# Pooled q and k of batches 1 to 3: column sums on TensorE against a matrix of ones, instead of VectorE reductions and transposes

## The chip, the cores and the metric

One NeuronCore of one Trainium2 chip runs the kernel. The metric is the device time of one execution in microseconds; the time before is the median of three runs. The profile is of one further execution, read from the hardware profiler.

## The reference, cut to what matters

Inputs q, k, v have the shape (4 batches, 8 heads, 576 positions, 64). The output passes through an attention layer and two feed-forward layers; the change is in the attention's downsampled half:

```python
q_d = q.reshape(B, H, Sd, 4, D).mean(axis=3)      # Sd = 144
k_d = k.reshape(B, H, Sd, 4, D).mean(axis=3)
v_d = v.reshape(B, H, Sd, 4, D).mean(axis=3)
out_d = softmax(q_d @ k_d.T / 8) @ v_d
out_up = np.repeat(out_d, 4, axis=2)
...
x = (out_up + out_local) as (2304 tokens, 512)
h = x @ w_in;   y = (s * relu(h)**2 + b) @ w_out
h = y @ w2_in;  out = (h - tanh(h)) @ w2_out
```

out_local is a softmax over the seven nearest positions.

## The kernel before, in words

The 2304 tokens of the first feed-forward layer are cut into eight units of 288 (unit u is half a batch). For each unit, 16 chunks of the hidden width run on TensorE: layer 1 into the PSUM tile ph (line 735), relu, square and a split into two float32r parts on ScalarE and VectorE (tiles gh and gl, lines 747 to 756), and layer 2 into acc (line 768). Every float32 product is three float32r matmuls, so a chunk is 24 dense matmuls of 128 rows, 128 columns and 288 tokens. The second feed-forward layer follows (lines 735 and 1016) and touches nothing of this change.

Attention of batch 0 runs at the start in a form of its own. For batches 1 to 3 it runs beside the dense matmuls of the units before: `local_items` (the seven-wide half: products on VectorE, GpSimd and ScalarE, lines 181, 186, 245, 249 and 257, then transposes of O into the tile xt at line 296, the sum with the upsampled half at line 314, and the split into xh and xl) and `down_items` (the downsampled half). A unit's first dense matmul needs its xh.

`down_items(b)` walks four pairs of heads hq. For each pair:

- `load` (line 336) issues on SyncE's queue two DMAs each for q, k and v into a tile `raw`: 72 partitions, each with four neighbouring positions of two heads, in pieces of 1 KB. One pool of two buffers holds q, k and v in turn.
- `padd` (line 345) sums the four positions: for q and k one VectorE reduction over the innermost of a rearranged view (line 353), for v two additions on GpSimd (lines 350 and 351). The sums are the tiles pp.
- `qkt` (line 368) transposes each pp by TensorE in two halves of 72 (line 375) into the PSUM tile qkps, and ScalarE copies it to qkT (lines 379 and 380).
- `scores`, `norm`, `ptr` and `pvm` make the 144 by 144 softmax and its product with v (tiles S, E, PT and up; lines 391 to 444) and fill upT.

The PSUM tiles qkps, S, PT, up and xt take turns in one pool of two banks (tag sd).

The items of the two lists are laid into the chunks' slots in program order. Batch 1's run in the last 18 or so slots ahead of unit 2, those of batches 2 and 3 over two units each. Then `list_schedule` (line 1260) sets the order of every engine's instructions from a table of costs and due times, and `pin_order` fixes it: each engine, and SyncE's queue, runs strictly in that order. The table prices a float32 matmul that is no transpose at 1.2 ns a moving column, a transpose at 64 or 110 ns, and a dense one at (columns + 32) / 2.4 ns (lines 1084 to 1094); a DMA's bytes start 1.3 us after its issue, flow at 300 GB/s, and have landed 0.9 us later (lines 1316 to 1321).

Of the kernel before, what the change touches and what calls it, by code (L numbers as in the profile page):

```python
# [7 lines left out]
F32 = mybir.dt.float32  # L8
# [3 lines left out]
ALU = mybir.AluOpType  # L12
AX = mybir.AxisListType.X

B, H, S, D = 4, 8, 576, 64
# [10 lines left out]
GH = G // 2  # L26
# [52 lines left out]
def attention_moe_moe_kernel(ctx: ExitStack, tc, q, k, v, w_in, w_out, s_in, b_in, w2_in, w2_out, out):  # L79
    nc = tc.nc  # L80
    pe, act, dve, pool, sp = nc.tensor, nc.scalar, nc.vector, nc.gpsimd, nc.sync

    sb = ctx.enter_context(tc.tile_pool(name="sb", bufs=1))
# [17 lines left out]
    ident = sb.tile([128, 128], F32, name="ident")  # L101
    caps = [sb.tile([128, TAU, NO], F32, tag=f"cap{h}", name=f"cap{h}") for h in range(2)]
    scal = sb.tile([128, 2], F32, name="scal")
    bcol = sb.tile([128, KC], F32, name="bcol")

    def emit_consts():
        pool.memset(ident, 0.0)
        pool.affine_select(out=ident, in_=ident, pattern=[[-1, 128]], compare_op=ALU.not_equal,
                           fill=1.0, base=0, channel_multiplier=1)

        band = g_p.tile([128, NB1], F32, tag="gl", name="band")[:QB, :KW + 6]
        pool.memset(band, 0.0)
        pool.affine_select(out=band, in_=band, pattern=[[1, KW + 6]], compare_op=ALU.is_ge,
                           fill=-BIG, base=-3, channel_multiplier=-1)
        pool.affine_select(out=band, in_=band, pattern=[[-1, KW + 6]], compare_op=ALU.is_ge,
                           fill=-BIG, base=9, channel_multiplier=1)
        b0["band"] = start.tile([QB, 1, KW + 6], F32R, name="bandr")
        b0["id"] = start.tile([QB, QB], F32R, name="identr")
        act.copy(out=b0["band"][:, 0], in_=band)
        act.copy(out=b0["id"], in_=ident[:QB, :QB])  # L120

        pool.memset(caps[0], FREE)
        for t in range(3):
            pool.memset(caps[0][0:4, t, 0:3 - t], MASKED)
        pool.memset(caps[1], FREE)
        c = caps[1][96:128]
        pool.affine_select(out=c, in_=c, pattern=[[-1, TAU], [-1, NO]], compare_op=ALU.is_ge,
                           fill=MASKED, base=11, channel_multiplier=0)
        pool.affine_select(out=c, in_=c, pattern=[[0, TAU], [0, NO]], compare_op=ALU.is_ge,
                           fill=FREE, base=-28, channel_multiplier=1)  # L130
# [201 lines left out]
    def down_items(b):  # L332
        it = []
        st = {}

        def load(hq):
            for nm, a in (("q", q), ("k", k), ("v", v)):
                base = (b * H + 2 * hq) * S * D
                t = raw_p.tile([128, 2, 2, 4, D], F32, tag="raw", name="raw72")
                for hf in range(2):  # L340
                    src = bass.AP(a.tensor, base + hf * GH * 4 * D, [[4 * D, GH], [S * D, 2], [1, 4 * D]])
                    sp.dma_start(out=t[:GH, hf].rearrange("p h r d -> p h (r d)"), in_=src)
                st[nm, hq] = t

        def padd(hq, nm):
            t = st[nm, hq]
            t2 = late.tile([GH, 2, 2, D], F32, tag="pp_" + nm, name="pp2")
            if nm == "v":
                t1 = t[:GH, :, :, 0:2, :]
                pool.tensor_tensor(out=t1, in0=t1, in1=t[:GH, :, :, 2:4, :], op=ALU.add)  # L350
                pool.tensor_tensor(out=t2, in0=t[:GH, :, :, 0, :], in1=t[:GH, :, :, 1, :], op=ALU.add)
            else:
                dve.tensor_reduce(out=t2.rearrange("p a h d -> p (a h) d").unsqueeze(3),
                                  in_=t[:GH].rearrange("p a h r d -> p (a h) d r"), axis=AX, op=ALU.add)
            st[nm + "p", hq] = t2

        def loads(hq):
            def f():
# [2 lines left out]

        def pools(hq):
            def f():
                for nm in "qkv":
                    padd(hq, nm)
            return f

        def qkt(hq):
            def f():
                if hq == 0:  # L370
                    upT[b] = late2.tile([128, 4, G], F32, tag="upT", name="upT")
                p_ = ps_sd.tile([128, 2, G], F32, tag="sd", name="qkps")
                for n, nm in enumerate("qk"):
                    for hf in range(2):
                        pe.transpose(p_[:, n, GH * hf:GH * hf + GH],
                                     st[nm + "p", hq][:, hf].rearrange("p h d -> p (h d)"), ident[:GH, :GH])
                t = late.tile([128, 2, G], F32, tag="qkT", name="qkT")

                act.activation(out=t[:, 0], in_=p_[:, 0], func=AF.Copy, scale=1.0 / 128.0)
                act.copy(out=t[:, 1], in_=p_[:, 1])  # L380
                st["T", hq] = t
            return f
# [345 lines left out]
    def l1(ph, p_, xh, xl, i):  # L728
        g, c = i // 4, (i % 4) * 128
        n = 0  # L730
        for kc in range(KC):
            w_h, w_l = wh[ph, "A", g, kc][:, c:c + 128], wl[ph, "A", g, kc][:, c:c + 128]
            x_h, x_l = (xh[kc], xl[kc]) if ph else (xh[:, kc], xl[:, kc])
            for w_, x_ in ((w_h, x_h), (w_h, x_l), (w_l, x_h)):
                pe.matmul(p_, w_, x_, start=n == 0, stop=n == 3 * KC - 1)  # L735
                n += 1
# [5 lines left out]
    def act1(key, p_):  # L742
        with ahead(P_ACT):
            act1_(key, p_)
# [14 lines left out]
    def l2_1(u, i):  # L759
        gh, gl = gt.pop((u, i))  # L760
        g, j = i // 4, i % 4
        first, last = next((i0, i1 - 1) for u_, i0, i1 in groups if u_ == u and i0 <= i < i1)
        if i == first:
            accs[u] = [ps_acc.tile([128, 512], F32, tag=f"acc{e}", name="acc") for e in range(4)]
        for e in range(4):
            w_h, w_l = (x[0, "B", g, j][:, 128 * e:128 * e + 128] for x in (wh, wl))
            for n, (w_, g_) in enumerate(((w_h, gh), (w_h, gl), (w_l, gh))):
                pe.matmul(accs[u][e][:, :g_.shape[1]], w_, g_, start=i == first and n == 0,  # L768
                          stop=i == last and n == 2)
# [59 lines left out]
    st1 = ExitStack()  # L829
    start3 = st1.enter_context(tc.tile_pool(name="start3", bufs=3))  # L830
    start2 = st1.enter_context(tc.tile_pool(name="start2", bufs=2))
    start = st1.enter_context(tc.tile_pool(name="start", bufs=1))
    emit_consts()
    b0_alloc()
    wn = {"l": 0, "s": 0}
# [6 lines left out]
    def w_done():  # L842
        n = wn["s"]
        if n < wn["l"]:
            w_split(0, n)
            wn["s"] += 1
# [55 lines left out]
    for u in range(2, NU):  # L902
        c = NF * u
# [7 lines left out]
    for s_, (n, u, i) in enumerate(seq):  # L911
        u_, i0, i1 = groups[n - 1]
        k_ = i - groups[n][1]
        if k_ == 0 and n:
            l2_1(u_, i1 - 2)
        if u == NU - 2 and i == CLOSE6:
            st1.close()
            st0.close()
            fin = ctx.enter_context(tc.tile_pool(name="fin", bufs=1, reuse_waits="tile"))
            yst_p = ctx.enter_context(tc.tile_pool(name="yst2", bufs=YB2, reuse_waits="tile"))  # L920
            fin2 = ctx.enter_context(tc.tile_pool(name="fin2", bufs=2, reuse_waits="tile"))
        p_ = ps_ph.tile([128, NB1], F32, tag="ph", name="ph")
        l1(0, p_, *X[u], i)
        act1((u, i), p_)
        if n and k_ == 1:
            l2_1(u_, i1 - 1)
            evac1(u_, None if u_ else n - 1 and 1)
        elif k_ >= LAG:
            l2_1(u, i - LAG)
        if u < 2:  # L930
            for _ in range(2 if s_ < HA else W_RATE):
                w_done()
        if s_ >= W2_SLOT0:
            w2_step(s_ - W2_SLOT0)
        for f in at[s_]:
            f()
        if s_ == HA - 1:
            st1.close()
            late = st1.enter_context(tc.tile_pool(name="late", bufs=1, reuse_waits="tile"))
            late2 = st1.enter_context(tc.tile_pool(name="late2", bufs=2, reuse_waits="tile"))  # L940
            yst_p = st1.enter_context(tc.tile_pool(name="yst", bufs=YB, reuse_waits="tile"))
            raw_p = st1.enter_context(tc.tile_pool(name="raw", bufs=2, reuse_waits="tile"))
        if s_ == HA:
            load_q(2)
            load_win(2, k, Kt, "K")
            load_win(2, v, Vt, "V")
# [94 lines left out]
    for j in range(last + 1):  # L1041
        for i in range(NF):
            p_ = ps_ph.tile([128, SIZES2[j]], F32, tag="ph", name="ph2")
# [341 lines left out]
```

## Time and profile before

| | us |
|---|---|
| median of three runs | 964.3 (964.13 to 965.61) |
| the profiled execution's own time | 967.31 |
| its span, first to last instruction | 965.5 |
| TensorE busy | 938.6 (97%) |
| VectorE busy | 596.7 (62%) |
| ScalarE busy | 456.2 (47%) |
| GpSimd busy | 154.7 (16%) |

Time outside the span is 1.8 us. Matmuls are pipelined: each one's record (about 290 ns for a dense one) overlaps the next, so a busy share says little about TensorE's pace. The pace is the distance between starts; a chain of waits lists stretches by it. "PEld" is the load of a matmul's stationary operand, "PEclk" the granted TensorE clock, where 1.00 is 2.4 GHz and 0.50 is 1.2 GHz. A float32 matmul that is no transpose leaves two records; a float32r one and a transpose leave one.

### The profile page before, as it was taken

How to read it: one execution, taken by the hardware profiler on the slowest of the kernel's cores; microseconds unless marked ns; L12 is line 12 of the kernel's file. 1: busy time of each engine (PE TensorE's matmuls, PEld its weight loads, DVE VectorE, ACT ScalarE, POOL GpSimd, SP SyncE). 2: the span in 40 equal slices, each digit the busy share in tenths (PEclk: the TensorE clock that was granted, in tenths of full speed). 3: DMA queues.
4: the chain of work that ended last, by engine and by line, in shares of the span. 5: the costliest groups of instructions: out<-in, count | busy, mean ns of one | idle time of the engine just before them, and what ended most of it. 6: DMA issues, size and time to landing. Idle time of an engine off the chain costs nothing.

```text
span 965.5 us, 15135 instructions
## 1 busy us (share of the span) xinstructions
PE 938.6 (97%) x5786; PEld 840.9 (87%) x5786; DVE 596.7 (62%) x966; ACT 456.2 (47%) x1216; POOL 154.7 (16%) x128
## 2 busy tenths in 40 slices
PE   7999999969999999999999999999999999999998
PEld 6888999959999999999999989888888888888886
DVE  4567899899899999988877963322322242222222
ACT  4679654635746565563777962212222131222211
POOL 1444342432312313131200000000000000000000
PEclk7559999988999999999999999999999999999999
DMA  9990052443113132301165750000110010001001
GB/s 225 313 351 14 26 168 63 127 127 115 52 65 114 60 110 78 110 7 41 47 234 221 270 155 1 23 1 1 44 43 1 1 33 12 0 1 44 1 1 43
DMA packets 57965, 80.71 MB, mean 84 GB/s; under 512 B 21046, under 2 KB 42790, under 8 KB 57894
## 3 DMA queue, kind: packets, MB, share of 16 engines
q1 hardware_dynamic: 57510, 79.24, 25.9%
q8 instruction: 45, 0.74, 0.3%
q10 hardware_dynamic: 384, 0.52, 0.2%
q14 instruction: 26, 0.21, 0.1%
HBM read 69.72 MB, written 10.03 MB: 83 GB/s over the span
## 4 chain that ended last, share of the span: by engine, by line
PE 75%; DVE 12%; ACT 7%; issue 3%; DMA 2%; SPq 1%; DVEq 0%; ACTq 0%
PE ph L735 34%; PE acc L1016 20%; PE acc L768 12%; ACT pA L245 2%; PE S L575 2%; DVE s L186 2%; DVE xq L314 1%; DVE pD L181 1%; PE O L598 1%; DVE gl L756 1%; DVE wf L715 1%; DMA wraw<-in_moe_w_in_dram 1%; DVE O L257 1%; SPq L502 1%; ACT E L401 1%
## 5 line engine op out<-in xcount | busy, mean ns | idle before, releaser
L735 PE MATMUL ph<-xh,w 128*128 128x288 f32 x1024 | 235.2, 304 | 2.8 <-DVE gl L756 2.1
L768 PE MATMUL acc<-gh,w 128*128 128x288 f32 (+1 forms) x1024 | 227.7, 298 | 1.5 <-DVE yst L791 0.9
L735 PE MATMUL ph<-yxh,w 128*128 128x512 f32 (+1 forms) x640 | 194.2, 369 | 0.6 <-DVE gl L1003 0.6
L1001 DVE TENSOR_TENSOR ph<-ph,th 128x512 f32<-128x512 f32 (+1 forms) x80 | 51.6, 645 | 224.4 <-ACT th L1000 224.4
L1016 PE MATMUL acc<-w,gx 128*128 128x512 f32 x768 | 185.4, 390 | 0.0
L735 PEld LDWEIGHTS ph<-xh,w 128*128 128x128 f32 x1024 | 174.0, 191 | 9.0 <-DVE gl L756 4.0
L768 PEld LDWEIGHTS acc<-gh,w 128*128 128x128 f32 x1024 | 171.4, 189 | 3.0 <-issue 1.7
L1016 PEld LDWEIGHTS acc<-w,gx 128*128 128x128 f32 x768 | 144.1, 188 | 31.2
L1000 ACT ACTIVATE th<-ph 128x512 f32<-128x512 f32 (+1 forms) x80 | 44.5, 556 | 233.1 <-PE ph L735 233.1
L735 PE MATMUL ph<-xl,w 128*128 128x288 f32 x512 | 154.4, 302 | 0.2 <-DVE xl L318 0.2
L768 PE MATMUL acc<-gl,w 128*128 128x288 f32 x512 | 151.5, 296 | 0.4 <-DVE gl L756 0.4
L735 PEld LDWEIGHTS ph<-yxh,w 128*128 128x128 f32 x640 | 116.9, 188 | 22.9 <-DVE gl L1003 1.3
L735 PE MATMUL ph<-yxl,w 128*128 128x512 f32 (+1 forms) x320 | 118.2, 369 | 0.0
L735 PEld LDWEIGHTS ph<-xl,w 128*128 128x128 f32 x512 | 97.9, 191 | 1.4 <-issue 0.6
L768 PEld LDWEIGHTS acc<-gl,w 128*128 128x128 f32 x512 | 96.6, 189 | 1.2 <-DVE gl L756 0.6
L747 ACT ACTIVATE ph<-ph 128x288 f32<-128x288 f32 x128 | 50.9, 398 | 94.8 <-PE ph L735 91.4
L756 DVE TENSOR_TENSOR gl<-ph,gh 128x288 fp32r<-128x288 f32 x128 | 57.6, 451 | 25.4 <-ACT gh L753 24.3
L735 PEld LDWEIGHTS ph<-yxl,w 128*128 128x128 f32 x320 | 60.2, 188 | 10.7
L1003 DVE TENSOR_TENSOR gx<-ph,gx 128x512 fp32r<-128x512 f32 x64 | 44.2, 691 | 37.9 <-ACT gx L1002 37.9
L1002 ACT CAST gx<-ph 128x512 fp32r<-128x512 f32 x64 | 37.6, 588 | 45.0 <-DVE ph L1001 44.9
L245 ACT ACTIVATE pA<-V,a 128x64 f32<-128x64 f32 x198 | 54.0, 342 | 9.8 <-DVE a L234 6.1
L753 ACT CAST gh<-ph 128x288 fp32r<-128x288 f32 x128 | 50.9, 399 | 5.7 <-PE acc L768 2.4
(137 smaller groups left out, 1203.7 us busy)
## 6 DMA issues: line engine op xcount, KB each, us to landing
wraw<-in_moe_w_in_dram SPq DMA_DIRECT2D x32, 512.0 KB
wraw<-in_moe_w_out_dram SPq DMA_DIRECT2D x32, 512.0 KB
y<-yst SPq DMA_DIRECT2D x36, 144.0 KB
K<-in_k_dram SPq DMA_DIRECT2D x5, 960.0 KB
V<-in_v_dram SPq DMA_DIRECT2D x5, 960.0 KB
Q<-in_q_dram SPq DMA_DIRECT2D x6, 576.0 KB
raw<-in_q_dram SPq DMA_DIRECT2D x24, 144.0 KB
raw<-in_k_dram SPq DMA_DIRECT2D x24, 144.0 KB
```

Source lines behind the costliest of these rows:

```text
L186: dve.tensor_reduce(out=st["s"][:, :, o:o + 1], in_=st[o].rearrange("p h t d -> p (h t) d"), axis=AX, op=ALU.add)
L245: act.activation(out=p_[:, t, h], in_=Vt[u][:, h, o + t], func=AF.Copy, scale=st["a"][:, h * TAU + t, o:o + 1])
L735: pe.matmul(p_, w_, x_, start=n == 0, stop=n == 3 * KC - 1)
L747: act.activation(out=p_, in_=p_, func=AF.Relu)
L753: act.copy(out=gh[:, :NB1], in_=p_)
L756: dve.tensor_tensor(out=gl, in0=p_, in1=gh[:, :NB1].bitcast(F32), op=ALU.subtract)
L768: pe.matmul(accs[u][e][:, :g_.shape[1]], w_, g_, start=i == first and n == 0, stop=i == last and n == 2)
L1000: act.activation(out=t, in_=p_, func=AF.Tanh)
L1001: dve.tensor_tensor(out=p_, in0=p_, in1=t, op=ALU.subtract)
L1002: act.copy(out=gh, in_=p_)
L1003: dve.tensor_tensor(out=gl, in0=p_, in1=gh.bitcast(F32), op=ALU.subtract)
L1016: pe.matmul(accs[j][t], g_, w_, start=i == 0 and n == 0, stop=i == NF - 1 and n == 2)
```

## The change

q and k of a head pair are loaded by position: 128 positions on the partitions, five blocks of them (the last of 64), two heads side by side, in pieces of 256 bytes, with three DMAs for each tensor. Each block is the stationary operand of a plain float32 matmul against `quad`, a constant with a one where position // 4 is the column. The result is the sum of four positions, already transposed, in qkps. The reductions at line 353, their tiles pp and the four transposes are gone. v keeps its way, with one raw buffer of its own; q and k share three.

```diff
+    quad = sb.tile([128, 32], F32, name="quad")
...
+        pool.memset(quad, 1.0)
+        pool.affine_select(out=quad, in_=quad, pattern=[[-4, 32]], compare_op=ALU.is_ge,
+                           fill=0.0, base=0, channel_multiplier=1)
+        pool.affine_select(out=quad, in_=quad, pattern=[[4, 32]], compare_op=ALU.is_ge,
+                           fill=0.0, base=3, channel_multiplier=-1)
...
         def load(hq):
-            for nm, a in (("q", q), ("k", k), ("v", v)):
+            for nm, a in (("q", q), ("k", k)):
                 base = (b * H + 2 * hq) * S * D
-                t = raw_p.tile([128, 2, 2, 4, D], F32, tag="raw", name="raw72")
+                t = raw_p.tile([128, 5, 2, D], F32, tag="rawt", name="raw128")
+                for h in range(2):
+                    src = bass.AP(a.tensor, base + h * S * D, [[D, 128], [128 * D, 4], [1, D]])
+                    sp.dma_start(out=t[:, :4, h], in_=src)
+                src = bass.AP(a.tensor, base + 512 * D, [[D, 64], [S * D, 2], [1, D]])
+                sp.dma_start(out=t[:64, 4], in_=src)
+                st[nm, hq] = t
+            for nm, a in (("v", v),):
+                base = (b * H + 2 * hq) * S * D
+                t = raw1_p.tile([128, 2, 2, 4, D], F32, tag="raw", name="raw72")
...
-                dve.tensor_reduce(out=t2.rearrange("p a h d -> p (a h) d").unsqueeze(3),
-                                  in_=t[:GH].rearrange("p a h r d -> p (a h) d r"), axis=AX, op=ALU.add)
...
                 for n, nm in enumerate("qk"):
-                    for hf in range(2):
-                        pe.transpose(p_[:, n, GH * hf:GH * hf + GH],
-                                     st[nm + "p", hq][:, hf].rearrange("p h d -> p (h d)"), ident[:GH, :GH])
+                    for c in range(5):
+                        np_ = min(128, S - 128 * c)
+                        pe.matmul(p_[:, n, 32 * c:32 * c + np_ // 4],
+                                  st[nm, hq][:np_, c].rearrange("p h d -> p (h d)"), quad[:np_, :np_ // 4],
+                                  start=True, stop=True)
...
-            raw_p = st1.enter_context(tc.tile_pool(name="raw", bufs=2, reuse_waits="tile"))
+            raw_p = st1.enter_context(tc.tile_pool(name="raw", bufs=3, reuse_waits="tile"))
+            raw1_p = st1.enter_context(tc.tile_pool(name="raw1", bufs=1, reuse_waits="tile"))
```

## Rows read from the trace of the kernel before

**Rows 1.** The page: busy time of each engine, share of the span, instructions.

```profile
PE 938.6 (97%) x5786; PEld 840.9 (87%) x5786; DVE 596.7 (62%) x966; ACT 456.2 (47%) x1216; POOL 154.7 (16%) x128
```

**Rows 2.** Busy time by stretch of batches 1 to 3, all engines.

```profile
core 0: us, PE busy (x) PEld busy (x) DVE busy (x) ACT busy (x) POOL busy (x), PEclk, DMA share, GB/s
130.00:205.70 75.70, 74.81 (x567) 69.57 (x566) 69.19 (x99) 38.18 (x128) 26.72 (x29) 1.00 0.33 104
205.70:217.66 11.96, 4.67 (x21) 3.15 (x19) 11.88 (x20) 3.14 (x7) 5.07 (x3) 0.71 0.50 156
217.66:224.30 6.64, 5.93 (x23) 5.24 (x24) 6.64 (x8) 3.33 (x12) 2.58 (x2) 0.50 0.27 89
224.30:433.00 208.70, 206.11 (x1602) 199.06 (x1601) 196.20 (x278) 124.84 (x421) 56.60 (x30) 1.00 0.25 80
433.00:436.30 3.30, 0.80 (x7) 0.56 (x5) 0.77 (x3) 2.50 (x10) 1.88 (x2) 0.95 0.00 0
436.30:440.00 3.70, 3.67 (x21) 3.62 (x22) 3.70 (x7) 1.58 (x4) 2.41 (x1) 0.59 0.82 264
```

**Rows 3.** TensorE in order of time, the gap ahead of unit 2: start, length, idle before.

```profile
210.97 1.94 PE L296 MATMUL xt<-ident,O 128*128 128x128 f32 x8 [4.94 <-DVE O L257]
...
217.66 0.85 PE L735 MATMUL ph<-xh,w 128*128 128x288 f32 x2 [0.55 <-ACT xh L317]
```

**Rows 4.** What TensorE and its weight loads waited for, 130 to 500 us.

```profile
PE PT L427 <- DVE E L415: 2.5, 1, 2.5
PE acc L768 <- DVE yst L791: 0.9, 1, 0.9
...
PEld ph L735 <- issue: 3.3, 17, 0.2
PEld ph L735 <- DVE gl L756: 3.2, 7, 0.8
...
PEld qkps L375 <- ACT E L401: 1.1, 1, 1.1
```

**Rows 5.** The chain of waits by stretches: TensorE's own pace at full clock.

```profile
121.99 3.20 PE acc L768 x24
...
137.57 0.13 PE qkps L375 x2
```

**Rows 6.** Groups by line and shape: busy us, mean ns, idle before.

```profile
L353 DVE TENSOR_REDUCE pp<-raw 72x256 f32<-72x1024 f32 x24 | 48.5, 2025 | 0.0
```

**Rows 7.** Plain float32 matmuls with 96 stationary columns, a burst at full clock.

```profile
115.51 0.82 PE L598 MATMUL O<-vw,bPT 102*96 102x65 f32 x8
```

**Rows 8.** By line: shortest, median, longest ns; starts. Stretches 85:120 and 130:222.

```profile
L598 PE MATMUL O<-vw,bPT x48: 220/248/248, 86.0 to 116.1; 102*96 102x65 f32 x48
...
L353 DVE TENSOR_REDUCE pp<-raw x11: 1948/2022/2048, 134.6 to 218.3; 72x256 f32<-72x1024 f32 x11
```

**Rows 9.** VectorE in order of time, ahead of unit 2.

```profile
209.48 1.34 DVE L257 TENSOR_TENSOR O<-O,pP 128x1152 f32<-128x1152 f32 x1
```

**Rows 10.** ScalarE and VectorE ahead of the wait at 436 us.

```profile
431.81 2.28 ACT L245 ACTIVATE pA<-V,a 128x64 f32<-128x64 f32 x9
...
435.53 0.46 DVE L756 TENSOR_TENSOR gl<-ph,gh 128x288 fp32r<-128x288 f32 x1 [3.11 <-ACT gh L753]
```

**Rows 11.** Loads of raw, what SyncE's queue waited for, GpSimd's wait, DMA rates.

```profile
L342 SPq DMA_DIRECT2D raw<-in_q_dram x24: 300/377/811, 130.2 to 369.6; - x24
...
SPq L342 <- DVE pp L353: 47.7, 12, 10.2
...
186.80 0.74 SPq L342 DMA_DIRECT2D raw<-in_v_dram  x2
190.48 1.99 POOL L350 TENSOR_TENSOR raw<-raw 72x512 f32<-72x512 f32 x1 [5.08 <-DMA raw<-in_v_dram]
...
0.00:20.00 20.00, 14.39 (x76) 12.45 (x77) 7.76 (x14) 8.61 (x14) 2.69 (x22) 0.82 1.00 226
60.00:70.00 10.00, 10.00 (x42) 7.86 (x42) 8.27 (x19) 6.45 (x17) 1.94 (x4) 0.50 1.02 390
```

More of the change, by code (lines that the diff above doesn't have):

```diff
@@ L343, in load, with padd @@
                 st[nm, hq] = t
[L345 to L352, printed above, removed]
-                dve.tensor_reduce(out=t2.rearrange("p a h d -> p (a h) d").unsqueeze(3),
-                                  in_=t[:GH].rearrange("p a h r d -> p (a h) d r"), axis=AX, op=ALU.add)
-            st[nm + "p", hq] = t2
+        def padd(hq):
+            t = st["v", hq]
+            t2 = late.tile([GH, 2, 2, D], F32, tag="pp_v", name="pp2")
+            t1 = t[:GH, :, :, 0:2, :]
+            pool.tensor_tensor(out=t1, in0=t1, in1=t[:GH, :, :, 2:4, :], op=ALU.add)
+            pool.tensor_tensor(out=t2, in0=t[:GH, :, :, 0, :], in1=t[:GH, :, :, 1, :], op=ALU.add)
+            st["vp", hq] = t2
         def loads(hq):
@@ L363, in f @@
             def f():
-                for nm in "qkv":
-                    padd(hq, nm)
+                padd(hq)
             return f
```

## The prediction

> **What bounds the kernel now.** I read the page first: TensorE is busy for 97% of the span, VectorE for 62% [rows 1]. That does not say that VectorE has room: the change acts only where batches 1 to 3 are prepared, from 130 to some 415 us, and there the table by stretch has VectorE busy 69.19 of 75.70 us, then 11.88 of 11.96, then 196.20 of 208.70 [rows 2]. So two engines stand near their limit at once, and the question is what TensorE loses to VectorE there, against what it is given to do.
>
> TensorE's pace comes from the chain of waits, where nothing is in its way: 24 dense matmuls in 3.20 us, 133 ns each; two transposes of pp in 0.13 us, 65 ns each [rows 5]. With these prices I went through the stretches for lost time. The largest hole is ahead of unit 2. From 205.70 to 224.30 us (18.60 us) TensorE started 44 matmuls [rows 2]: even at the dense price that is 5.9 us, and about 4.7 us, an estimate, with the small ones among them priced by kind. Some 13.9 us are lost. The order of time shows how: the transposes of O wait 4.94 us for VectorE's last addition into O, the first dense matmul comes at 217.66, and the clock is down to 0.50, 1.2 GHz, until 224.30 [rows 2, 3]. VectorE was busy throughout, and that last addition came at 209.48 [rows 9].
>
> Elsewhere little is lost. Of 130 to 205.70 all but 0.89 us is busy, of 224.30 to 433 all but 2.59 us [rows 2]. One more hole is from 433.00 to 440.00: 28 matmuls in 7.00 us, 3.7 us at 133 ns, so 3.3 us or a little more lost, the clock again halved in its second part [rows 2]. Its wait is put down to VectorE [rows 4], but VectorE itself had sat idle for 3.11 us until ScalarE, in a run of products pA, came to the relu and split of the chunk [rows 10]. VectorE's load is not its cause.
>
> **The change part by part.**
>
> *VectorE.* 24 reductions of 2025 ns go, 48.5 us [rows 6]. They are worth what TensorE waited for them, not 48.5 us. Eleven of them start between 134.6 and 218.3 us [rows 8], ten ahead of the last addition into O, so that can come up to 20 us sooner. The hole ahead of unit 2 should all but close: even with no help from VectorE, TensorE would come to it some 8 us later than now, by its added work of batch 1. I leave about 0.9 us of it for the hand-over from xt to xh and take 13.0 us as returned. Of the small waits I count those that end on a late VectorE: 0.9 for yst; 1.1 of the wait of qkps, since it now waits for no reduction; and half of the 3.2 for gl [rows 4]: 3.6 us. Of the hole at 433 us I count half, 1.7 us, since the order of ScalarE is made anew. TensorE being later by 2 us a pair also covers some short waits that do not hang on its own last chunk: 1.2 us, an estimate. Sum returned: 19.5 us. Bounds: 13.0 if only the first hole closes; 27 if the second hole, all of gl and the 3.3 us of issue gaps [rows 4] go as well.
>
> *TensorE.* 48 transposes of 65 ns go, 3.1 us. 24 tensors of five blocks are 120 float32 matmuls, 240 records. No row has 128 stationary columns and 32 moving ones as float32 at full clock, so I bound the price. The nearest is line 598, 96 stationary and 65 moving columns: eight records in 0.82 us, the last one 0.248 us long, so (0.82 - 0.248) / 7 = 82 ns a record [rows 7, 8]. If the load of the stationary operand sets that, 128 columns give 82 x 128 / 96 = 109 ns. The lower end is the transpose of pp, which also loads 128 columns, at 65 ns [rows 5]; the upper end is a dense matmul with its 288 moving columns, 133 ns. I take 109 ns: like line 598 these are plain float32, two records each, and no transposes. Sum: 240 x 0.109 = 26.2 us (15.6 to 31.9), net of the transposes **+23.1 us** (12.5 to 28.8). All of it is on the path, since TensorE has next to no idle time to put it in; where it falls into the hole ahead of unit 2, that hole is already counted as returned in full.
>
> The Trainium skill, TensorE: Matmul & The Clock Gate, section LDWEIGHTS, gives a load as the number of columns over 1.2, in ns: an estimate of 80 ns for 96 columns and 107 ns for 128. The 82 ns of line 598 agree, the 65 ns of the transposes, also with 128 columns, do not; by the rule the net is 22.6 us, by the transposes' price 12.5 us.
>
> *Loads.* q and k take three DMAs instead of two: 24 more issues of 0.38 us on SyncE's queue, 9 us spread over 285 us. The pieces shrink from 1 KB to 256 bytes. 24 tensors of 288 KB are 7.1 MB: at the 390 GB/s of one fully busy stretch 18 us of all DMA engines, at the 226 GB/s of another, with small pieces among its loads, 31 us [rows 11]. The 13 us between them fit into a DMA share of 0.25 to 0.33 [rows 2]. Nothing is counted; with that cover gone it would show as the landing rival below.
>
> *Waits that move.* The loads of raw waited 47.7 us for reductions [rows 11]; now a k or q load waits for the matmuls of an earlier tensor, with a third buffer to hide it. A v load, with one buffer, waits for GpSimd's second addition; behind it in SyncE's queue stand stores of y and the next q, k and windows. A pair takes 16 us or more, a load 3.7 us from issue at 186.80 to use at 190.48 [rows 11], so I count nothing. On TensorE the ten matmuls of a pair wait for a load instead of VectorE, with dense matmuls behind them. The bank of qkps is held for about 2.2 us, as before, when its two transposes stood a reduction of 2.0 us apart. The constant is three short GpSimd instructions in the first 20 us, where GpSimd is busy for 2.69 us [rows 11]: nothing. SBUF costs no time.
>
> *Sum.* +23.1 - 19.5 = +3.6 us. The profiled execution took 967.31 us, 3.0 above the median, so it goes to 970.9, and the median of 964.3 to **967.8**.
>
> **The rivals.**
>
> *Faster: the second half of the waits was VectorE's too.* Place: the split gl of each chunk and the scaling E ahead of PT, which stand in VectorE's order behind products of 1.3 us and more. Deciding point: whether the hole at 433 us closes whole and gl's waits all go; then returns reach 27 us, and the time is 964.3 + 23.1 - 27 = 960.4 (958 to 962.4). For it: VectorE at 94% in 224 to 433 us [rows 2]. Against: ScalarE ahead of the larger wait [rows 10]. Chance 0.18.
>
> *Faster: the load is cheap.* If 128 columns cost 65 ns outside a transpose, the net is 12.5 us and the time 964.3 + 12.5 - 19.5 = 957.3. Against: line 598 took 82 ns for fewer columns [rows 7]. Chance 0.07.
>
> *No change: it only cancels.* Returns of 21 to 25 us against 23.1. Chance 0.15; time 964.3.
>
> *Slower by the clock.* A burst of 20 records streams only 32 columns each. If the clock falls to 1.2 GHz as it did when TensorE stood waiting, dense work runs slower behind it: 3.7 us near half speed in the second hole [rows 2], some 1.9 us lost, and the burst itself doubles, 2.2 us. At four of twelve bursts that is 16 us: 984; at two, 976. Against: the runs of small matmuls at 224 to 433 us left it at 1.00 [rows 2]. Chance 0.07.
>
> *Slower by landings.* The planner counts 2.2 us and the bytes for a load, and TensorE's order is strict, so a late load of q or k stops the dense matmuls behind it. Price: up to 3.7 us [rows 11] a time, at three pairs 8 to 11 us: 976 to 979. It decides where a load is issued less than one pair ahead. The Trainium skill, DMA: Bandwidth & Descriptors, Specifications, puts line rate at transfers of 512 B or more; the new pieces are half that. No row here prices such a piece alone. Chance 0.08.
>
> **How the numbers follow.** Two medians of this kernel can be told apart at about 0.2%, 1.9 us. The forecast, 0.45, has its own range of 965 to 972. Faster: 0.18 + 0.07, and 0.01 for orders not thought of: 0.26. Same: 0.15, and 0.05 from the forecast's lower edge: 0.20. Slower: 0.40 + 0.07 + 0.08, less that 0.01: 0.54. The range holds the forecast, the cancelling case, both faster cases and the milder halves of the last two: 957 to 977.
>
> **What would show it.** No reductions on VectorE at the pooled sums, its busy time down by 48 us; 120 new matmuls at 105 to 115 ns a record; the first dense matmul of unit 2 at 205 to 212 us instead of 217.66, with the clock at 1.00; unit 2 starting earlier by 6 to 12 us, and that lead lost again by 2 us a pair until 420 us. I am wrong if the records stand 65 ns apart, if TensorE waits for raw, if the clock falls in the bursts, or if the lead at unit 2 is kept to the end.

## The result, and the profile after

The changed kernel takes 977.27 us, median of four runs (974.26 to 978.47), against 964.89 us before (four runs, 964.13 to 965.61). The ratio is 1.0124, 95% interval 1.0097 to 1.0151: slower by 12.4 us. The forecast of 967.8 us had the direction and less than a third of the size; the upper end of its range, 977, lies 0.3 us under the median; the forecast started from 964.3, 0.6 us under the kernel before as it ran beside the changed one. The profiled execution took 978.47 us, its span is 976.7 us, 11.2 us longer than before.

The page of the changed kernel, the lines that answer to [rows 1], with the chain that ended last and the granted clock in 40 slices:

```profile
span 976.7 us, 15500 instructions
...
PE 964.1 (99%) x5978; PEld 869.4 (89%) x5978; DVE 555.5 (57%) x942; ACT 457.3 (47%) x1216; POOL 153.6 (16%) x131
...
PEclk7559998999999999999999999999999999999999
...
PE 91%; DVE 4%; ACT 1%; issue 1%; DMA 1%; SPq 1%; DVEq 0%; ACTq 0%
```

The chain of the kernel before:

```profile
PE 75%; DVE 12%; ACT 7%; issue 3%; DMA 2%; SPq 1%; DVEq 0%; ACTq 0%
```

VectorE has lost 41 us of busy time and 8 points of the chain (12% before); TensorE is all but the whole chain now (91% against 75%). So the relief did what it was made for, and the question is what TensorE pays. One slice of PEclk inside the dense part is an 8. Asked stretch by stretch, the trace shows five places from 130 to 435 us, none of which the kernel before has (columns as in [rows 2]):

```profile
148.15:151.56 3.41, 3.41 (x16) 3.41 (x16) 1.64 (x3) 0.91 (x4) 0.00 (x0) 0.51 0.54 121
168.63:172.04 3.41, 3.41 (x17) 3.41 (x16) 3.11 (x6) 2.88 (x12) 0.88 (x1) 0.51 0.50 113
301.75:305.16 3.41, 3.41 (x15) 3.41 (x15) 2.67 (x2) 1.88 (x8) 3.41 (x1) 0.51 0.79 168
349.53:352.95 3.42, 3.42 (x17) 3.42 (x16) 1.33 (x2) 1.56 (x5) 0.00 (x0) 0.51 0.53 124
370.01:373.43 3.42, 3.42 (x19) 3.36 (x17) 2.04 (x2) 0.98 (x4) 0.00 (x0) 0.51 0.65 147
```

Each is a fall of the granted clock to 1.2 GHz for 3.41 us (0.51 is the mean of the stretch), with TensorE busy all through. What stands ahead of one is seen in order of time, TensorE alone (start, length, line, count):

```profile
165.05 0.29 PE L781 MATMUL acc<-gh,w 128*128 128x290 f32 x1
165.19 2.62 PE L387 MATMUL qkps<-quad,raw 128*128 128x32 f32 x20
167.74 0.40 PE L748 MATMUL ph<-xh,w 128*128 128x288 f32 x1
...
168.51 0.52 PE L748 MATMUL ph<-xh,w 128*128 128x288 f32 x2
168.83 0.44 PE L748 MATMUL ph<-xl,w 128*128 128x288 f32 x1
169.07 0.68 PE L748 MATMUL ph<-xh,w 128*128 128x288 f32 x2
```

The ten matmuls of a pair of heads run as one burst of 20 records (in two of the twelve pairs other matmuls stand between, after 4 records at 224.1 us and after 8 at 276.3 us). Less than a microsecond after it, in the middle of dense matmuls, the distance of two starts goes from 0.13 to 0.24 us. All five places lie 0.9 us or less behind such a burst; there are twelve bursts. At 0.51 of the clock a stretch of 3.41 us loses 1.67 us: five are **8.4 us**.

A sixth fall stands in the second feed-forward layer, which the change doesn't touch, behind a wait of 1.87 us for ScalarE. It costs 1.7 us:

```profile
577.68 0.73 PE L1030 MATMUL acc<-w,gh 128*128 128x512 f32 x2 [1.87 <-ACT gh L1016]
...
578.30:581.71 3.41, 3.41 (x16) 3.22 (x16) 0.42 (x2) 1.33 (x2) 0.00 (x0) 0.50 0.87 253
```

The burst's own cost is read from the chain, where it stands without its overlap with the next matmul:

```profile
165.35 2.46 PE qkps L387 x20
...
185.12 2.47 PE qkps L387 x20
```

Twelve of 2.46 us are 29.5 us; with the 3.1 us of transposes [rows 5] gone, **+26.4 us** net. The hole ahead of unit 2 [rows 2, 3] is closed: between 205.70 and 224.30 us TensorE is busy in every microsecond, at full clock, and the first dense matmul of unit 2 waits for nothing:

```profile
219.97 0.53 PE L748 MATMUL ph<-xh,w 128*128 128x288 f32 x2
...
205.70:224.30 18.60, 18.60 (x140) 16.84 (x139) 15.61 (x29) 9.24 (x28) 3.21 (x3) 1.00 0.41 116
224.30:433.00 208.70, 208.41 (x1582) 202.74 (x1582) 174.18 (x261) 121.84 (x407) 64.38 (x30) 0.98 0.28 85
433.00:440.00 7.00, 7.00 (x60) 6.62 (x59) 6.90 (x7) 2.69 (x8) 0.74 (x1) 1.00 0.01 2
```

Yet it starts 2.3 us later than before, at 219.97 against 217.66 [rows 3]: four bursts of batch 1, a fifth of batch 2 and two of the slow stretches stand in front of it. What TensorE still waits for from 120 to 515 us is 0.7 us, and with its weight loads it has no reduction, no O and no raw in it, and of E one wait of 0.2 us, the answer to [rows 4]:

```profile
PE acc L781 <- ACT yst L802: 0.4, 1, 0.4
PE ph L748 <- DVE xl L325: 0.3, 1, 0.3
...
PEld ph L748 <- issue: 3.7, 19, 0.2
...
PEld ph L748 <- DVE gl L769: 0.8, 4, 0.2
```

The account of the two profiled executions is then: +26.4 for the matmuls, +8.4 for the five falls, +1.7 for the sixth, and, since the total is +11.2, 25.3 us returned. That last figure is a remainder; it holds waits, and what the kernel before lost at half clock ahead of unit 2 and at 436 us [rows 2].

### The profile page after: what moved, and what is told of

It reads as the page before. It is cut to its first block, busy times and chain, and to the rows that moved or that the text cites. A ratio compares the mean times of both kernels' runs of the same rounds, so it can differ in the third digit from the quotient of the medians.

```text
span 976.7 us, 15500 instructions
## 1 busy us (share of the span) xinstructions
PE 964.1 (99%) x5978; PEld 869.4 (89%) x5978; DVE 555.5 (57%) x942; ACT 457.3 (47%) x1216; POOL 153.6 (16%) x131
## 3 DMA queue, kind: packets, MB, share of 16 engines
q1 hardware_dynamic: 78822, 79.24, 26.4%
## 4 chain that ended last, share of the span: by engine, by line
PE 91%; DVE 4%; ACT 1%; issue 1%; DMA 1%; SPq 1%; DVEq 0%; ACTq 0%
PE ph L748 40%; PE acc L1030 20%; PE acc L781 18%; PE qkps L387 3%; PE S L588 2%; PE O L611 1%; PE warm L866 1%; PE up L455 1%; SPq L515 1%; DVE s L193 1%; PE S L404 1%; PE Sd L627 1%; PE PT L601 1%; PE PT L440 1%; DVE O L264 1%
## 5 line engine op out<-in xcount | busy, mean ns | idle before, releaser
L748 PE MATMUL ph<-xh,w 128*128 128x288 f32 x1024 | 238.0, 307 | 0.6 <-DVE gl L769 0.6
L748 PEld LDWEIGHTS ph<-xh,w 128*128 128x128 f32 x1024 | 176.0, 193 | 6.1 <-issue 3.3
L256 POOL TENSOR_TENSOR pP<-V,a 128x1152 f32<-128x1152 f32 x12 | 35.8, 2986 | 119.0 <-DVE O L264 66.8
```

The lines of the kernel that those rows point to most:

```text
L256: eng.tensor_tensor(out=p_, in0=Vt[u][:, :, o:o + TAU, :].rearrange("p h t d -> p t h d"), in1=aw.to_broadcast([128, TAU, 2, D]), op=ALU.mult)
```

## The experiments

The theory A: the loss is TensorE's added time plus the falls of the clock, with some 20 us of waits returned. The rivals: B, the added time alone (the slow stretches do not count); C, late loads in pieces of 256 bytes. Times are medians of one submission, beside the kernel before on the same chip.

**What the relief is worth by itself.** Two kernels take the price away. One leaves VectorE's reductions out of the kernel before:

```diff
+            if nm != "v":
+                st[nm + "p", hq] = t[:GH, :, 0, 0:2, :]
+                return
...
-            else:
-                dve.tensor_reduce(out=t2.rearrange("p a h d -> p (a h) d").unsqueeze(3),
-                                  in_=t[:GH].rearrange("p a h r d -> p (a h) d r"), axis=AX, op=ALU.add)
```

> The kernel before with the 24 reductions of q and k left out: TensorE transposes the first two positions' worth of the raw tile instead, so the pooled sums of q and k are left out, the loads and transposes are as before. This is the most that taking the reductions from VectorE can return at no price. Theory A: 20 to 22 us, 943 to 945 us, about 3 us below the one-block kernel. Rival (returns are small and the rest of the loss is elsewhere): 950 us or more.

The other is the changed kernel with one block of five, which streams 144 columns of a zero-padded `quad`:

```diff
-                    for c in range(5):
+                    for c in range(1):
...
-                        pe.matmul(p_[:, n, 32 * c:32 * c + np_ // 4],
-                                  st[nm, hq][:np_, c].rearrange("p h d -> p (h d)"), quad[:np_, :np_ // 4],
-                                  start=True, stop=True)
+                        pe.matmul(p_[:, n], st[nm, hq][:np_, c].rearrange("p h d -> p (h d)"),
+                                  quad[:np_, 128 - 32 * c:128 - 32 * c + G], start=True, stop=True)
```

> The changed kernel with one of the five blocks of each tensor multiplied (against 144 zero-padded columns); four fifths of the pooled sums of q and k are left out. Loads are unchanged. Theory A: TensorE's price falls from 26.9 to 24 x 2 x 0.12 = 5.8 us (3.1 us of transposes gone), no falls, about 21 us of waits returned: 964.9 + 2.7 - 21 = 946 to 948 us. If the waits returned were only 12 us: 955 to 957 us. Rival C (loads): 965 us or more, with TensorE waiting for raw.

Measured: 950.25 us without the reductions and 950.56 us with one block, against 965.31. So the reductions alone hold up 15.1 us (ratio 0.9845, 0.9828 to 0.9861), not the 20 to 22 expected. Both numbers missed: one block by 2.6 us or more; without the reductions by 5.3 us or more, inside the range of that run's rival (950 or more), and not 3 us under the other. The two kernels differ in the layout and buffers of the loads, with pieces of 1 KB in one and 256 bytes in the other, and in the price of 24 short matmul pairs; they take the same time. Loads in small pieces show no cost here, and rival C falls.

The 25.3 us of the account is more than 15.1. The one-block kernel pays 12 x 0.49 us on the chain for its matmuls, 2.8 net of the transposes, and its span is 16.7 us shorter than before, so 19.5 us come back in it (2 to 3 us of that because the profiled execution before lies above its median by that much). From it to the changed kernel the price rises by 12 x (2.46 - 0.49) = 23.6 us and six falls cost 10.1, 33.7 together, while the span grows by 27.9. Most of the 5.8 us between is idle time that TensorE still has in the one-block kernel and fills with matmuls in the changed one, 5.6 against 0.7 us:

```profile
130.00:435.00 305.00, 299.43 (x2309) 286.61 (x2308) 267.69 (x408) 181.65 (x608) 102.88 (x64) 1.00 0.31 92
130.00:435.00 305.00, 304.27 (x2289) 292.47 (x2289) 250.34 (x377) 166.95 (x555) 95.02 (x62) 0.97 0.31 91
```

**The clock, first try.** The same loads of the stationary operand, but 144 moving columns instead of 32:

```diff
-                        pe.matmul(p_[:, n, 32 * c:32 * c + np_ // 4],
-                                  st[nm, hq][:np_, c].rearrange("p h d -> p (h d)"), quad[:np_, :np_ // 4],
-                                  start=True, stop=True)
+                        pe.matmul(p_[:, n], st[nm, hq][:np_, c].rearrange("p h d -> p (h d)"),
+                                  quad[:np_, 128 - 32 * c:128 - 32 * c + G], start=c == 0, stop=c == 4)
```

> The changed kernel, but each block's matmul streams all 144 columns of a zero-padded matrix of ones and accumulates, so the number of loads of the stationary operand is the same and only the moving columns grow, from 32 to 144. Reference values: before 964.9, changed 977.3. Theory A (the added 26 us on TensorE are paid in full, about 20 us of waits come back, and the rest of the loss is the clock falling after five of the twelve bursts, some 7 to 8 us): records go from 112 to about 122 ns, +2.4 us, no stretch at 0.50 begins behind a burst, 971 to 973 us. Rival B (the loss is TensorE's added work alone, the falls beside it cost nothing that counts): 979 to 980 us. Rival C (late loads in pieces of 256 bytes hold TensorE): 977 to 980 us, as the loads are unchanged.

Measured: 977.08 us (ratio 1.0122, 1.0107 to 1.0137), where A said 971 to 973; the range of C, 977 to 980, holds it. The stretch from 130 to 435 us, in the wide kernel, at full clock:

```profile
130.00:435.00 305.00, 303.65 (x2291) 286.26 (x2290) 247.32 (x379) 166.96 (x557) 91.45 (x59) 1.00 0.30 90
```

and its bursts on the chain:

```profile
164.26 3.30 PE qkps L387 x20
...
183.34 3.04 PE qkps L387 x20
```

No slow stretch is left there, as A has it; but a burst is now 3.04 us long instead of 2.46 (the 3.30 holds a wait), 7 us in twelve, and that ate most of the gain. I had priced the pace at 122 ns, which the trace has, and not the longer stops inside the burst. By its time alone this run decides nothing.

**The clock, second try.** The same matmuls in two halves with dense ones between:

```diff
+            if hq < 3:
+                it.append((0, qkt(hq + 1, 0)))
             it.append((0.8, norm(hq)))
...
-                it.append((0, qkt(hq + 1)))
+                it.append((0, qkt(hq + 1, 1)))
```

The last argument is 0 for q and 1 for k; each half writes a PSUM tile of its own.

> The changed kernel with the ten matmuls of a pair of heads cut in two: q's five in one item and k's five in a later one, each with a PSUM tile of its own, dense matmuls between. Same work. Theory A: bursts of 1.1 us in place of 2.4 us, at most one or two falls of the clock behind them, 969 to 972 us. Rival B (added work alone): 976 to 979 us, whatever the clock does. Rival C (late loads): 976 to 979 us.

Measured: 972.87 us (971.51 to 977.38; ratio 1.0086, 1.0061 to 1.0112), 4.4 us below the changed kernel, a little over A's upper end and outside the ranges of B and C. The halves are 1.14 us long on the chain (one of the four shown by the profile between 155 and 200 us is 1.40), so their work is the same, and the clock of its profiled execution is 1.00:

```profile
130.00:435.00 305.00, 302.92 (x2331) 289.93 (x2331) 258.64 (x380) 170.00 (x561) 93.13 (x63) 1.00 0.31 91
```

The two intervals overlap by a little, so the time speaks for A without proof; the clock is plain. Only about half of what the falls cost came back; TensorE is idle 1.4 us more than in the changed kernel's row, and the rest isn't taken apart.

**The stops inside a burst.** In the changed kernel's trace a record follows the last within 0.11 us except around the fifth block, the one of 64 positions, where the distances are 0.21, 0.13 and 0.19 us. Two kernels remove the 64-row block. The first fills it with positions already covered:

```diff
-                src = bass.AP(a.tensor, base + 512 * D, [[D, 64], [S * D, 2], [1, D]])
-                sp.dma_start(out=t[:64, 4], in_=src)
+                src = bass.AP(a.tensor, base + 448 * D, [[D, 128], [S * D, 2], [1, D]])
+                sp.dma_start(out=t[:, 4], in_=src)
...
+                        x = quad if c < 4 else quad[:, 16:]
+                        pe.matmul(p_[:, n, 32 * c:32 * c + 32 if c < 4 else G],
+                                  st[nm, hq][:, c].rearrange("p h d -> p (h d)"), x, start=True, stop=True)
```

> The changed kernel with the last block of each tensor filled to 128 rows (positions 448 to 575; the moving matrix is zero or beside the wanted columns for the rows that belong to the fourth block, whose columns are not touched). Still ten blocks and 240 records a batch set, q and k in one burst; only the switch between 128 and 64 rows is gone. Theory A: 4.6 us of edges go, bursts shrink from about 2.55 to 2.25 us. If the falls stay (five, 7 us): 972 to 974 us. If a burst of this length no longer brings one: 964 to 967 us, about 3 us above the kernel with nine blocks. Rival (edges are nothing): 976 to 978 us.

Measured: 966.39 us (ten runs, 965.04 to 968.01; ratio 1.0006, 0.9995 to 1.0017): 10.9 us off, with the same count of matmuls, moving columns and reloads, and inside the 964 to 967 that were expected if no fall were left. A burst, and the stretch of the bursts:

```profile
162.78 2.14 PE qkps L387 x20
...
130.00:435.00 305.00, 303.70 (x2383) 292.64 (x2383) 261.63 (x400) 172.36 (x576) 95.36 (x63) 1.00 0.32 93
```

2.14 us instead of 2.46 is 3.8 us in twelve bursts. The clock stays at 1.00, and the rest, 7 us, is what the falls cost: 3.8 + 8.4 = 12.2 by the account, 10.9 by the two medians. This is the run that B cannot explain: the added time is cut by 3.8 us and the loss by nearly three times that.

That the rest is the clock, and not another order of waits, can be read unit by unit. A unit is taken from its first dense matmul to that of the next, in us; the price is 0.32 us a burst and 1.67 us a fall:

| unit | before | changed | bursts, falls in it | full rows | changed less full rows | price |
|---|---|---|---|---|---|---|
| 1 | 81.5 | 82.0 | 4, 2 | 77.2 | 4.8 | 4.6 |
| 2 | 57.6 | 56.2 | 1, 0 | 55.8 | 0.4 | 0.3 |
| 3 | 59.2 | 65.3 | 2, 1 | 62.8 | 2.4 | 2.3 |
| 4 | 57.9 | 63.4 | 2, 2 | 60.3 | 3.1 | 4.0 |
| 5 | 64.4 | 63.1 | 2, 0 | 62.4 | 0.7 | 0.6 |

The difference stands where the falls were, in each unit within 0.9 us of the price. The table also shows where the change loses: 11.6 us in units 3 and 4, where TensorE had little idle time before [rows 2].

The granted clocks of all runs agree. In the changed kernel the slower a run, the lower its granted clock: 978.47 us at 0.960, 978.32 at 0.962, 976.21 at 0.964, 974.26 at 0.966. One less that clock, times the span, is 36.1 us on average there, 28.9 in the ten runs with full rows and 29.2 in the wide and in the split kernel's: some 7 us more in the changed kernel, as much as the rest above. An average over the span hides this beside the kernel before, whose runs have 0.956 to 0.965: there the clock was halved around the hole ahead of unit 2, in part while TensorE waited [rows 2].

The second puts the last 64 positions of q and of k side by side in one block of 128 rows, nine blocks instead of ten:

```diff
+            tl = tail_p.tile([128, 2, D], F32, tag="rawe", name="rawe")
...
+                sp.dma_start(out=tl[64 * n:64 * n + 64], in_=src)
...
+                pe.matmul(p_[:, :, 128:], st["e", hq].rearrange("p h d -> p (h d)"), quad, start=True, stop=True)
```

> The changed kernel with the last 64 positions of q and of k side by side in one block of 128 rows: nine blocks in place of ten, none with 64 rows. In the changed kernel's trace a block of 64 rows takes 192 ns more than the pace at its two edges, 4.6 us in all, so theory A (price first): 24 records fewer, 2.7 us, and 4.6 us of edges: 7 us off; the bursts are still 2.0 us long, and one to five falls stay: 967 to 972 us. Rival (the edges are hidden anyway): 974 to 977 us.

Measured: 962.55 us (ratio 0.9964, 0.9950 to 0.9978), faster than before and 4 to 9 us better than A expected, and no fall was left behind any burst. On the chain a burst is 1.71 + 0.22 us:

```profile
160.37 1.71 PE qkps L388 x16
162.07 0.22 PE qkps L390 x2
...
130.00:435.00 305.00, 304.19 (x2390) 293.04 (x2389) 264.00 (x400) 176.48 (x593) 96.61 (x61) 1.00 0.31 90
```

12 x (2.46 - 1.93) = 6.4 us of price and 8.4 us of clock make 14.8; measured 977.27 - 962.55 = 14.7. That the two agree so closely is partly luck: in the second layer the changed kernel's profiled execution has its sixth fall, and that of this kernel is at half clock for 6.8 us from 560.5 us on, behind a wait of 2.68 us.

**Both cures at once, a miss.** Nine blocks, and q's in an earlier item, in the same PSUM tile:

```diff
+            if hq < 3:
+                it.append((0, qkt(hq + 1, 0)))
             it.append((0.8, norm(hq)))
```

> The kernel with nine blocks of 128 rows, and q's matmuls in an earlier item than k's and the shared block's: price and falls taken off together. Theory A: 7 us for the blocks and 4 to 8 us for the falls, bursts of 0.9 and 1.1 us with no fall behind them: 962 to 966 us, the same as before the change. Rival (the two do not add up, because something else holds TensorE): 969 us or more.

Measured: 976.64 us, 14 us slower than nine blocks in one burst. TensorE starts 2277 records between 130 and 435 us where that kernel starts 2390, and it waits for what that kernel does not wait for:

```profile
130.00:435.00 305.00, 297.28 (x2277) 284.11 (x2276) 253.48 (x376) 168.06 (x558) 93.27 (x62) 0.99 0.31 90
...
PE PT L444 <- DVE E L432: 1.6, 3, 0.8
PE PT L444 <- DVE xq L321: 1.4, 2, 0.8
PE up L459 <- issue: 1.3, 1, 1.3
```

TensorE is idle for 7.7 us there, where that kernel's is idle for 0.8, and two falls cost 3.4; the rest of the 14 isn't found. One of the two banks of the tag sd is now held from q's matmuls to k's, a slot or more later, and PT, up and xt have to go through the other; the earlier split kernel gave each half a tile of its own. That is a likely reason of the waits, but it is argued: no run gives this kernel a third bank.

**The planner's price.** One number of its table, set to what a record pair takes:

```diff
-            t = 1.2 * n
+            t = 240.0 if n in (16, 32) else 1.2 * n
```

> The changed kernel with one number of the planner's table set right: matmuls of 16 and 32 columns cost it 240 ns in place of 19 and 38, so the order of all engines is made for the true price. The instructions are the same. Theory A (work on TensorE, edges and falls make the loss, not the order): 974 to 980 us. Rival (the order, made for a price six times too low, makes a good part of the loss): 965 to 971 us.

Measured: 976.80 us (973.52 to 979.02), the changed kernel's time. The order made for a price of 38 ns instead of 240 costs nothing that can be measured.

**Cheaper matmuls.** Each block's heads apart, 64 stationary columns each, into the two halves of the partitions:

```diff
-                        pe.matmul(p_[:, n, 32 * c:32 * c + np_ // 4],
-                                  st[nm, hq][:np_, c].rearrange("p h d -> p (h d)"), quad[:np_, :np_ // 4],
-                                  start=True, stop=True)
+                        for h in range(2):
+                            pe.matmul(p_[64 * h:64 * h + 64, n, 32 * c:32 * c + np_ // 4],
+                                      st[nm, hq][:np_, c, h], quad[:np_, :np_ // 4], start=True, stop=True)
```

> The changed kernel with each block's two heads multiplied apart: two matmuls of 64 stationary columns, into partitions 0 to 63 and 64 to 127, in place of one of 128. Same sums, same loads. If the load of the stationary operand is the price and loads to different column halves overlap, as in the kernel before at line 644 (64 columns, two records 8 ns apart, the pair 63 ns), TensorE pays 24 x 5 x 2 x 0.063 = 15 us in place of 31 us, bursts shrink to 1.3 us and few falls of the clock are left: theory A gives 953 to 960 us. If the halves do not overlap (rival), each record costs about 60 ns, twice as many of them, and the time stays at 974 to 979 us.

Measured: 963.02 us (ratio 0.9965, 0.9951 to 0.9980), above A's range by 3 us and far from the rival's. The stops of the 64-row block are still in it. Without them, in nine blocks:

> Nine blocks of 128 rows, each block's two heads multiplied apart with 64 stationary columns. Records stand 59 ns a pair in the kernel with ten blocks and heads apart, so a pair of heads takes 9 x 2 x 0.059 = 1.1 us, 12.7 us in all, in place of some 31 us. Theory A: 6 to 7 us below that kernel's 963.0, 955 to 958 us, level with the two additions on VectorE (957.4). Rival (what is left is not TensorE's price): 961 us or more.

Measured: 956.93 us (ratio 0.9895, 0.9871 to 0.9919), as expected. On the chain a burst shrinks from 1.62 us (ten blocks) to 1.05 + 0.12 us (nine):

```profile
162.87 1.62 PE qkps L388 x40
```

```profile
160.79 1.05 PE qkps L389 x32
161.84 0.12 PE qkps L392 x4
```

**The same relief without TensorE.** Two additions instead of the reduction, nothing else:

```diff
-                dve.tensor_reduce(out=t2.rearrange("p a h d -> p (a h) d").unsqueeze(3),
-                                  in_=t[:GH].rearrange("p a h r d -> p (a h) d r"), axis=AX, op=ALU.add)
+                t1 = t[:GH, :, :, 0:2, :]
+                dve.tensor_tensor(out=t1, in0=t1, in1=t[:GH, :, :, 2:4, :], op=ALU.add)
+                dve.tensor_tensor(out=t2, in0=t[:GH, :, :, 0, :], in1=t[:GH, :, :, 1, :], op=ALU.add)
```

> The kernel before with each reduction of q and k (2.03 us) replaced by two additions on VectorE, of 512 and 256 elements, some 0.6 and 0.4 us: VectorE gives back about 24 us of the 48.5 and TensorE does nothing new. Theory A (what counts is VectorE's time up to a point, and the one hole ahead of unit 2 takes the larger part of it): 8 to 13 us faster than before, 952 to 957 us. Rival (additions on VectorE hold up GpSimd's, and the hole stays): 961 us or more.

Measured: 957.38 us (953.90 to 958.25; ratio 0.9907, 0.9885 to 0.9929), a little over A's upper end. The rows that answer to [rows 6]:

```profile
L354 DVE TENSOR_TENSOR raw<-raw 72x512 f32<-72x512 f32 x24 | 20.7, 864 | 1.6 <-DMA raw<-in_q_dram 1.6
...
L355 DVE TENSOR_TENSOR pp<-raw 72x256 f32<-72x256 f32 x24 | 9.9, 414 | 0.0
```

30.6 us instead of 48.5: 18 us less on VectorE gave 8.6 us. I had expected about 24 us less. This and the heads apart in nine blocks beat both kernels of the case, and cannot be told from each other.

## Why the prediction was right or wrong, step by step

*Which engine bounds: right.* Two engines near their limit, VectorE's relief worth only what TensorE waited, the hole ahead of unit 2 closed, the rest of the sum on TensorE's path. VectorE's busy time is down by 41 us rather than 48: the reductions are gone, and other instructions take 7 us more.

*The price of a record: right. The price of a burst: too low.* I took 109 ns; a block of 128 rows follows the last at 112 ns in a burst, and the 20 records of the kernel with full rows stand on the chain with 2.14 us, 107 ns each. (The steady distance in [rows 7] is 85 ns, only the first is shorter; by the same rule of three it gives 113 ns.) The step that failed is "240 x 0.109": 48 of the 240 belong to blocks of 64 rows, and these stop the burst at both edges, 0.32 us a burst. Net +26.4 us instead of +23.1.

The Trainium skill, TensorE: Matmul & The Clock Gate, section LDWEIGHTS, gives columns over 1.2, an estimate of 107 ns for 128 columns, and says that the row count does not matter. The trace agrees with the first where rows do not change, at 107 to 112 ns; the 0.32 us a burst that the change of rows costs speaks against reading the second as free of cost between neighbours.

*The waits returned: on the low side.* 19.5 us summed, 25.3 us by the account (bounds were 13 to 27; the terms named for the upper one add up to 26). The reductions' own part is 15.1 us, measured alone. TensorE's added work covers some 5 to 6 us more of waits, as the one-block kernel shows, where I had allowed 1.2 us. "All of it is on the path" was wrong by that much.

*The clock: the step that failed.* "Slower by the clock" stood among the rivals with a chance of 0.07, and its mechanism came true beside the forecast's, not in its place. I argued against it with small matmuls that had left the clock at 1.00 [rows 2]; the longest I had looked at ran for 0.82 us [rows 7]. Its price was mis-sized too: 4 us a fall, of which 1.9 by the second hole, where TensorE had been standing still, and 2.2 for a burst at half clock, which no burst was; 1.67 us measured. The rival's "at two, 976" comes near the measured time by luck, too few falls at too high a price, and the range reached to 977 by it and by late landings, which did not come. The sum of +3.6 us stands against 11.2 us between the two profiled executions, 7.6 us short: five falls are 8.4 us, the sixth 1.7, the bursts 3.3 more than summed, and 5.8 more came back. The last three all but cancel, so the clock is the miss.

*Unit 2 earlier by 6 to 12 us: wrong.* It starts 2.3 us later. I put the lead at the hole and the payment behind it; in fact two fifths of the bursts and two of the falls stand ahead of unit 2.

*Loads, SyncE's queue, GpSimd: right to count nothing.* SyncE waits 70.5 us for the new matmuls where it waited 47.7 us for reductions [rows 11], and TensorE waits for no raw:

```profile
SPq L349 <- PE qkps L387: 70.5, 11, 21.9
```

The Trainium skill, DMA: Bandwidth & Descriptors, Specifications, puts line rate at transfers of 512 B or more. At a DMA share of 0.31, far from full, the pieces of 256 bytes made no difference of time between the two kernels without the price.

## What to carry to other kernels

Work moved from an engine that is nearly the bound to the one that is the bound returns only the waits (15 us of 48.5 here) and pays nearly all of its price; first make it cheap where it is, or cheap where it goes. A burst of small float32 matmuls was paid here mostly by the columns of its stationary operand (112 ns a record with 32 moving columns, 122 with 144), so cut these in halves that overlap, and keep the rows of neighbours equal. A price list of single instructions misses what a burst does to the clock of the work behind it: look at the granted clock behind the longest burst of the kind, and if the trace has none that long, treat the fall as a term of the sum.

## What the runs showed of the hardware that was not expected

The clock fell behind bursts of 2.46 us with 32 moving columns and the stops of the 64-row blocks, in five of twelve cases of the profiled execution, while TensorE counted as busy throughout. It did not fall behind bursts of 2.14 us with 32 columns and no stops (none in the profiled execution; ten runs within 3 us, at clocks of 0.967 to 0.971), nor behind bursts of 3.04 us with 144 columns. Each of these falls lasted 3.41 us. Their count differs from run to run: the changed kernel's four runs have granted clocks from 0.960 to 0.966, the slowest run the lowest. The kernel with the planner's price, which has the same matmuls, points the same way: its profiled execution has two falls, each behind a burst of 2.46 or 2.47 us, took 973.52 us and had a clock of 0.969, while its other three runs had 0.962 to 0.966 and took 975.79 to 979.02 us.

Not every fall in these traces stands behind a burst. The kernel with the heads of ten blocks apart has one, at 214.5 us, behind a burst of 1.62 us and a wait of 0.56 us for ScalarE; the kernel of nine blocks in two halves has two, behind waits of TensorE of 1.25 and 1.30 us; the one without reductions has one, behind a wait of 2.36 us for VectorE; the one with the two additions has one, at 267.2 us, behind two waits of 0.55 and 0.51 us, with no burst at all. The changed and the wide kernel have one each in the second layer, behind waits of 1.87 and 1.99 us. In the wide, the split and the full-row kernel, and in both of nine blocks in one burst, none stands behind a burst. What in a burst decides is therefore open: length alone does not, since 3.04 us with 144 columns left the clock up.

Changing from a stationary operand of 128 rows to one of 64 and back costs a burst with two such blocks 0.32 us on the chain. Two matmuls with 64 stationary columns into different halves of the partitions take three fifths of the time of one with 128: 1.17 us (1.05 + 0.12) for nine blocks apart against 1.93 us together.
